# Attention in channel layout from inputs laid out by the host, one scan per tile, and a clamp moved to another engine: one core of a Trainium2 chip

## The chip, the core and the metric

The kernel runs on one core of one Trainium2 chip. TensorE (PE) does the matrix products into PSUM, VectorE (DVE), ScalarE (ACT) and GpSimd (POOL) the elementwise work, and the queue of SyncE (SP) issues most of the transfers between HBM and SBUF. The metric is the device time of the kernel in microseconds; lower is better.

## The reference

Three parts follow each other; the output of each feeds the next.

```python
# 1. attention: 4 batches, 8 heads, 768 steps, head size 48; w between 0.8 and 0.95
for t in range(768):
    cur = einsum('bhd,bhe->bhde', u * k[t], v[t])
    y[t] = einsum('bhd,bhde->bhe', r[t], state + cur)
    state = w[t][..., None] * state + einsum('bhd,bhe->bhde', k[t], v[t])
# 2. FFN on x = y as (3072 tokens, 384); w_in 384x2048 and w_out 2048x384 come as float64
h = x @ w_in
g = where(h > 0, h, exp(min(h, 0)) - 1)
x = g @ w_out
# 3. mixture of 8 experts (384 -> 1024 -> 384, ReLU), each token to its best one, times its gate weight
```

## The kernel before, in words

**Attention.** The 24 tiles are 6 chunks of 128 steps times 4 batches; tile `i` is chunk `i // 4` of batch `i % 4`. A tile runs in four steps. `A1` takes the decays with tokens on partitions, turns them with three fp32 transposes on PE (L356) into channels on partitions (128 channels, three blocks), forms running products over the later half of the chunk forwards and over the earlier half backwards in six scans of 64 columns on DVE (L359, L360), and from these the reciprocals (Ln and Exp on ACT, L367 and L368; two Newton steps, L370 and L371). It forms the product r·k·u on POOL (L382, L384), sums it by head on DVE (L385), multiplies it into v (L392) and splits v and a scaled v into fp16 high and low halves (L346 and L347). `A2` turns the decay products back with six fp32 transposes (L434, L436), multiplies them with r and k (DVE L462, in early tiles ACT L459 and POOL L460), splits these into fp16 halves (L465 and L343), makes a copy of k with the halves exchanged (L478, L479) and has three DMA transposes per tile put them with channels on partitions (RT, KT, KS). `A3` forms the scores (L507, L508), masks them (L524) and splits them (L525, L343); `A4` forms y (L551 to L553), adds what the state gives (L561, L562), hands y to the FFN as fp16 halves, and brings the state `US` up to date (L590, L597). The decay of the state over a chunk goes through `dmh` and small matmuls (L376, L377, L440, L444). The first four tiles (`EAR`) run in fp32 without DMA transposes (extra fp32 transposes, L472); tiles below `NAV` = 6 keep scores, v and the update in fp32.

**FFN.** Six groups of four tiles. `ffn_in` has 16 blocks `m` of 128 hidden channels, each of nine matmuls of 512 tokens (L608); behind each comes the ELU: `e = exp(h)` on ACT (L613), clamp and scale on DVE (L614), `max` with `h` on DVE (L615), the fp16 high half on ACT (L616), the low half on POOL (L343, `gg<-e,gg`). `ffn_out` has 192 matmuls (L628). While group g runs, the attention steps of the tiles of group g+1 are woven in; within a first group there is nothing to weave in but the start, whose four tiles follow the string `ORD`. In the first group the float64 weights are also rebuilt: three integer steps on DVE (L292 to L294), two on ACT (L306, L309), one on POOL (L310) for each of 8 + 8 pieces.

**Experts.** Blocks of 256 tokens, loaded by token number, with weights loaded per block (`SG`, `wi`) and split by ACT (L941) and DVE (L942).

A scheduler sets the order of the instructions on each engine from this program; every engine then works its list in that order and waits at semaphores. The lists of both kernels are quoted below.

Of the kernel before, what the change touches and what calls it, by code (L numbers as in the profile page):

```python
# [99 lines left out]
def _consts():  # L100
# [8 lines left out]
    d = i[None, :] - i[:, None] - 1  # L109
    put("mask", np.where(d >= 0, RHO ** np.maximum(d, 0).astype(np.float64), 0.0) * 2.0 ** (SA - 2 * SR))  # L110
    put("rt", (RHO ** (i - 128.0) * 2.0 ** (SX - SR - PG - KS_))[:, None])
    put("rv", (RHO ** (127.0 - i) * 2.0 ** SG)[:, None])
# [18 lines left out]
def body(ctx, tc, r, k, v, w, u, w_in, w_out, mod, w_gate, bias, w1, w2, cst, out, dbg=None):  # L131
# [38 lines left out]
    ubc = p1.tile([128, DM], F32, name="ubc")  # L170
    cst1 = p1.tile([128, 1], F32, name="cst1")
    cstc = cst1.to_broadcast([128, 64])
    RKs = [p1.tile([128, 2, KD, 129], F32, name=f"RK{i}") for i in range(2)]
    KXs, RXs = ([t[:, q] for t in RKs] for q in range(2))
    Rt = [p1.tile([128, H, 128], F16, name=f"Rt{i}") for i in range(2)]
    Kt = [p1.tile([128, H, 128], F16, name=f"Kt{i}") for i in range(2)]
    K2s = [p1.tile([128, H, 128], F16, name=f"K2{i}") for i in range(2)]
# [1078 lines left out]
```

## Time and profile before

| what | value |
|---|---|
| median of 3 runs | 854.38 us (853.51 to 857.72) |
| the profiled execution | 853.07 us, of which 850.8 us span from first to last instruction |
| busy in the span | PE 752.4 us (88%), DVE 607.7 (71%), ACT 488.4 (57%), POOL 394.2 (46%) |
| first `ffn_in` matmul | 65.1 us |
| first `ffn_out` | 157 us |
| later groups begin | 255.0, 343.7, 432.0, 520.9 us |
| last `ffn_in` | 545.4 to 577.6 us |
| experts | from 666 us to the end |

A busy share over the whole span mixes stages with different limits, so the rows below go by stage. Idle time of an engine matters only where another waits for what it would have done.

### The profile page before, as it was taken

How to read it: one execution, taken by the hardware profiler on the slowest of the kernel's cores; microseconds unless marked ns; L12 is line 12 of the kernel's file. 1: busy time of each engine (PE TensorE's matmuls, PEld its weight loads, DVE VectorE, ACT ScalarE, POOL GpSimd, SP SyncE). 2: the span in 40 equal slices, each digit the busy share in tenths (PEclk: the TensorE clock that was granted, in tenths of full speed). 3: DMA queues.
4: the chain of work that ended last, by engine and by line, in shares of the span. 5: the costliest groups of instructions: out<-in, count | busy, mean ns of one | idle time of the engine just before them, and what ended most of it. 6: DMA issues, size and time to landing. Idle time of an engine off the chain costs nothing.

```text
span 850.8 us, 17360 instructions
## 1 busy us (share of the span) xinstructions
PE 752.4 (88%) x6395; PEld 492.0 (58%) x6395; DVE 607.7 (71%) x1351; ACT 488.4 (57%) x1079; POOL 394.2 (46%) x397
## 2 busy tenths in 40 slices
PE   3797667899899989998999999999898799999974
PEld 2683344465456645664566455545575577777753
DVE  5659999557986699569955985297488686775751
ACT  4566667345674567455754563254474586776751
POOL 6637779635684468645763664001103622421110
PEclk9678878899999999999999899999999899999998
DMA  9937675265447453673475232115946999999920
GB/s 213 216 94 164 140 167 156 44 113 94 111 83 115 94 105 73 128 105 81 77 118 119 62 48 51 31 38 170 288 158 233 312 330 250 291 239 265 268 74 12
DMA packets 258147, 121.83 MB, mean 143 GB/s; under 512 B 221989, under 2 KB 239562, under 8 KB 258052
## 3 DMA queue, kind: packets, MB, share of 16 engines
q1 hardware_dynamic: 253728, 109.75, 55.8%
q0 software_dynamic: 3456, 10.24, 4.0%
q8 instruction: 54, 0.88, 0.4%
q10 hardware_dynamic: 868, 0.62, 0.3%
q14 instruction: 41, 0.34, 0.1%
HBM read 81.63 MB, written 9.84 MB: 108 GB/s over the span
## 4 chain that ended last, share of the span: by engine, by line
PE 33%; DVE 28%; issue 10%; DMA 10%; ACT 5%; POOL 3%; SPq 0%; POOLq 0%; DVEq 0%; ACTq 0%
PE psf L628 15%; DVE e L614 6%; PE psa L970 6%; DMA out_dram<-ob,idxb 5%; DVE e L615 4%; PE psf L950 4%; PE psf L608 3%; DMA SG<-in_moe_w_dram 3%; PE psa L950 1%; POOL gg L343 1%; DVE gb L347 1%; DVE af L524 1%; DVE W L942 1%; DVE Ab L343 1%; DVE vb L347 1%
## 5 line engine op out<-in xcount | busy, mean ns | idle before, releaser
L608 PE MATMUL psf<-xT,wi 128*128 128x512 f16 x864 | 208.6, 395 | 27.0 <-DVE sti L294 16.0
L628 PE MATMUL psf<-wo,gg 128*128 128x384 f16 x1152 | 197.2, 327 | 2.2 <-ACT gg L616 1.5
L608 PEld LDWEIGHTS <-wi 128*128 128x128 f16 x864 | 85.0, 101 | 127.2 <-issue 42.3
L628 PEld LDWEIGHTS <-gg 128*128 128x128 f16 x1152 | 110.0, 98 | 72.5 <-ACT gg L616 1.8
L343 POOL TENSOR_TENSOR gg<-e,gg 128x512 f16<-128x512 f32 x80 | 96.6, 1210 | 41.2 <-ACT gg L616 34.2
L970 PE MATMUL psa<-W,gg 128*128 128x384 f16 x624 | 106.4, 331 | 3.0 <-DVE gg L343 3.0
L950 PEld LDWEIGHTS <-W 128*128 128x128 f16 x1008 | 93.6, 99 | 19.6 <-issue 7.2
L614 DVE TENSOR_SCALAR e<-e 128x512 f32<-128x512 f32 x96 | 81.8, 852 | 17.3 <-ACT e L613 16.2
L616 ACT ACTIVATE gg<-e 128x512 f16<-128x512 f32 x96 | 60.2, 627 | 55.1 <-DVE e L615 54.8
L970 PEld LDWEIGHTS <-gg 128*128 128x128 f16 x624 | 61.5, 99 | 43.8 <-DVE gg L343 3.5
L942 DVE SCALAR_TENSOR_TENSOR W<-SG,W 128x768 f16<-128x768 f32 x56 | 52.8, 955 | 31.7 <-ACT W L941 28.0
L613 ACT ACTIVATE e<-psf 128x512 f32<-128x512 f32 x96 | 56.4, 589 | 20.6 <-POOL gg L343 12.8
L941 ACT ACTIVATE W<-SG 128x768 f16<-128x768 f32 x56 | 45.9, 836 | 37.3 <-DMA SG<-in_moe_w_dram 34.1
L615 DVE SCALAR_TENSOR_TENSOR e<-e,psf 128x512 f32<-128x512 f32 x96 | 65.0, 678 | 1.0
L942 DVE SCALAR_TENSOR_TENSOR W<-wi,W 128x768 f16<-128x768 f32 x56 | 52.3, 954 | 18.6 <-ACT W L941 14.5
L950 PE MATMUL psf<-XM,W 128*128 128x256 f16 (+1 forms) x540 | 59.5, 267 | 6.8 <-DMA XM<-G 4.9
L978 POOL DMA_INDIRECT out_dram<-ob,idxb x20 | 22.8, 1140 | 87.0 <-DVE gg L343 29.9
L941 ACT ACTIVATE W<-wi 128x768 f16<-128x768 f32 x56 | 45.4, 836 | 25.6 <-PE psa L970 15.5
L343 DVE TENSOR_TENSOR gg<-mt,gg 128x256 f16<-128x256 f32 (+1 forms) x112 | 42.1, 401 | 18.1 <-ACT gg L957 15.9
L957 ACT ACTIVATE gg<-mt 128x256 f16<-128x256 f32 (+1 forms) x112 | 40.7, 397 | 1.2
L343 POOL TENSOR_TENSOR Rt<-rkn,Rt 128x384 f16<-128x384 f32 x20 | 19.6, 980 | 42.3 <-ACT Rt L465 42.0
L956 ACT ACTIVATE mt<-psf 128x256 f32<-128x256 f32 (+1 forms) x84 | 29.2, 364 | 16.5 <-DVE gg L343 10.2
(316 smaller groups left out, 1419.2 us busy)
## 6 DMA issues: line engine op xcount, KB each, us to landing
SG<-in_moe_w_dram SPq DMA_DIRECT2D x28, 768.0 KB
wi<-in_moe_w_dram SPq DMA_DIRECT2D x28, 768.0 KB
stg<-in_moe_w_in_dram SPq DMA_DIRECT2D x8, 768.0 KB
stg<-in_moe_w_out_dram SPq DMA_DIRECT2D x8, 768.0 KB
scr<-X SPq DMA_DIRECT2D x6, 770.0 KB
lw<-in_w_dram SPq DMA_DIRECT2D x24, 192.0 KB
lr<-in_r_dram SPq DMA_DIRECT2D x24, 192.0 KB
lk<-in_k_dram SPq DMA_DIRECT2D x24, 192.0 KB
```

The costliest lines, as they stand in the source:

```text
L343: (nc.gpsimd if pool else nc.vector).tensor_tensor(lo, f, hi, op=ALU.subtract)
L608: nc.tensor.matmul(ph, lhsT=wi[:, a, kk, c0:c0 + 128], rhs=xg[:, b_ * KD + kk, :], start=(n == 0), stop=(n == 3 * KD - 1))
L613: nc.scalar.activation(e, ph, AF.Exp, scale=_pow2(-PH))
L614: nc.vector.tensor_scalar(e, e, 1.0, _pow2(PH), op0=ALU.min, op1=ALU.mult)
L615: nc.vector.scalar_tensor_tensor(e, e, -_pow2(PH), ph, op0=ALU.add, op1=ALU.max)
L616: nc.scalar.activation(gg[:, 0, m, 0:w_], e, AF.Copy)
L628: nc.tensor.matmul(po[:, 0:DM], lhsT=gg[:, a, m, 128 * i:128 * i + 128], rhs=wo[:, b_, m, :], start=(m == 0 and a + b_ == 0), stop=(m == N ...
L941: nc.scalar.activation(o_[:, 0], i_, AF.Copy, scale=_pow2(sc))
L942: nc.vector.scalar_tensor_tensor(o_[:, 1], i_, _pow2(sc), o_[:, 0], op0=ALU.mult, op1=ALU.subtract)
L950: nc.tensor.matmul(ph[:, 0:n_], lhsT=w_[:, a, kk, 128 * m:128 * m + 128], rhs=xm[:, b_ * KD + kk, 0:n_], start=(n == 0), stop=(n == 3 * KD ...
L957: nc.scalar.activation(h2[:, 0, m, 0:n_], t_, AF.Copy)
L970: nc.tensor.matmul(po[:, 0:DM], lhsT=h2[:, a, m, 128 * t:128 * t + 128], rhs=w_[:, b_, m, :], start=(m == 0 and a + b_ == 0), stop=(m == N ...
```

## The change

Attention now works with channels on partitions from the start. The host delivers r, k and w of a tile as 112 partitions (48 channels of heads 0 to 3, 16 duplicated ones, 48 channels of heads 4 to 7) by 4 head pairs by 128 steps; w has a zero column ahead of each row and its earlier half reversed. The weights of FFN and experts are laid out so that each partition reads one contiguous stretch. What the steps are now:

- `A1`: ACT doubles every fifth decay (L324); one scan of 520 columns on DVE gives all running products (L325, a vector of zeros and ones restarts it); Ln and Exp (L328, L329) and two Newton steps (L330, L331), 512 columns wide. The state's decay is one small DVE operation (L334). POOL forms r·k (L341). From tile 8 on v is split (ACT L314, DVE L315).
- `A2`: products with r and k, in two halves of 256 columns each: POOL in tiles 0 to 7 (L371), DVE afterwards (L376). PE transposes k once in fp32 (four, L381) for the update, and four small fp32 matmuls with u give the r·k·u sums (L384). From tile 8 on fp16 halves of k and r (ACT L394, POOL L311). No DMA transposes, no exchanged copy.
- `A3`, `A4`: matmuls of 48 channels that alternate between the two partition groups; three fp16 products where there were two for scores and state; y gets what the state gives in two DVE operations of 192 columns (L475); the update is 8 fp32 matmuls instead of 32 fp16 ones.
- ELU: DVE L614 goes; ACT does scale and bias instead (L514), and DVE's one operation takes `min` and `max` (L515).
- `NAV` rises from 6 to 8, and `ORD` changes.

```diff
 def A1(i):
-        for j in range(KD):
-            nc.tensor.transpose(pw[:, 128 * j:128 * j + 128], wf[:, 128 * j:128 * j + 128], cc("ident"))
-        for j in range(KD):
-            nc.vector.tensor_tensor_scan(RX[:, j, 65:129], pw[:, o + 64:o + 128], cstc, 1.0, op0=ALU.mult, op1=ALU.mult)
-            nc.vector.tensor_tensor_scan(
-                KX[:, j, 0:64][:, ::-1], pw[:, o:o + 64][:, ::-1], cstc, 1.0, op0=ALU.mult, op1=ALU.mult
+        nc.scalar.activation(lw[:, DB0::DBL], lw[:, DB0::DBL], AF.Copy, scale=2.0)
+        nc.vector.tensor_tensor_scan(flat(PR), lw, bnd, 0.0, op0=ALU.mult, op1=ALU.add)
...
-        nc.gpsimd.tensor_tensor(rk, rk, ubc, op=ALU.mult)
-        nc.vector.tensor_reduce(dg, rk.rearrange("p (h d) -> p h d", h=H), axis=AX.X, op=ALU.add)
 def A2(i):
+            if i < NAV:
...
+                for t_, xv in parts:
+                    nc.gpsimd.tensor_tensor(f[:, :, t_], xv, st[nm][:, :, t_], op=ALU.mult)
             else:
...
+                for t_, xv in parts:
+                    nc.vector.scalar_tensor_tensor(f[:, :, t_], xv, _pow2(SR), st[nm][:, :, t_], op0=ALU.mult, op1=ALU.mult)
...
+                nc.tensor.transpose(pk[:, PT * s_:PT * s_ + PT], xs[0][:, s_, :], cc("ident")[0:PT, 0:PT])
...
+            nc.tensor.matmul(pk[:, o:o + H], lhsT=st["rk"][:, s_, :], rhs=usel[:, s_, :], start=(s_ == 0), stop=(s_ == QH - 1))
...
-        transp(KT, K1.rearrange("p h x -> p (h x)"), i < NPT)
-        transp(RT, R.rearrange("p h x -> p (h x)"), i < NPT)
-        transp(KS, K2.rearrange("p h x -> p (h x)"), i < NPT)
 def ffn_in(g, m):
         nc.scalar.activation(e, ph, AF.Exp, scale=_pow2(-PH))
-        nc.vector.tensor_scalar(e, e, 1.0, _pow2(PH), op0=ALU.min, op1=ALU.mult)
-        nc.vector.scalar_tensor_tensor(e, e, -_pow2(PH), ph, op0=ALU.add, op1=ALU.max)
+        nc.scalar.activation(e, e, AF.Identity, scale=_pow2(PH), bias=nel)
+        nc.vector.scalar_tensor_tensor(e, e, 0.0, ph, op0=ALU.min, op1=ALU.max)
...
-    ORD = '00 01 10 P 02 11 P 03 12 P 20 13 30 21 31 P 22 32 P 23 33'.split()
+    ORD = '00 01 10 P 02 11 20 P 03 12 21 30 P 13 22 31 P 23 32 33'.split()
```

Three places of the engines' lists follow. The first is DVE within an `ffn_in` stretch of a middle group (`e` is the block's ELU value, `gb` the split scaled v, `RK` the decay products, `US` the state). Before:

```order
L614 TENSOR_SCALAR e<-e 128x512
L597 SCALAR_TENSOR_TENSOR US_103<-US_103,psa 112x384
L565 SCALAR_TENSOR_TENSOR y<-psa,y 128x384
L615 SCALAR_TENSOR_TENSOR e<-e,psf 128x512
L347 SCALAR_TENSOR_TENSOR gb<-lv,cs,gb 128x384
L359 SCALAR_TENSOR_TENSOR RK_92<-psa,cst_90 128x64
L360 SCALAR_TENSOR_TENSOR RK_92<-psa,cst_90 128x64
```

The same kind of place on DVE now (`rkn` is a decay product times k or r, `lw` the decays as loaded):

```order
L497 SCALAR_TENSOR_TENSOR US_98<-US_98,psa 112x192
L330 SCALAR_TENSOR_TENSOR RK_93<-RK_93,psa 112x8x64
L331 SCALAR_TENSOR_TENSOR RK_93<-RK_93,psa 112x8x64
L325 SCALAR_TENSOR_TENSOR RK_93<-lw,bnd 112x520
L376 SCALAR_TENSOR_TENSOR rkn<-RK_93,lk 112x4x64
L376 SCALAR_TENSOR_TENSOR rkn<-RK_93,lr 112x4x64
L334 SCALAR_TENSOR_TENSOR dmc<-RK_93,Z_103 112x4
L515 SCALAR_TENSOR_TENSOR e<-e,psf 128x512
```

L614 and the gb split are gone, the six short scans (two of them shown) are one long one, and the new scan and L376 read both operands from SBUF (`RK`, `lw`, `bnd`, `lk`, `lr`), where the scans read one from PSUM (`psa`).

The second place is POOL shortly ahead of the first FFN block (`wi` is a rebuilt weight piece, `x` and `ohp` the low half of y, `gg` a spare region that holds products). Before:

```order
L460 TENSOR_TENSOR gg<-gg,lr 128x8x48
L384 TENSOR_TENSOR X_99<-X_99,ubc 128x384
L460 TENSOR_TENSOR gg<-gg,lk 128x8x48
L310 TENSOR_TENSOR wi<-sti,wi 128x3x256
L392 TENSOR_TENSOR ohp<-ohp,dg 128x384
L572 TENSOR_TENSOR x<-y,x 128x384
```

POOL at the same place now (`Tk` and `Tr` belong to tiles of the next group):

```order
L371 TENSOR_TENSOR Tk<-RK_93,lk 112x4x64
L341 TENSOR_TENSOR rk<-lr,lk 112x512
L371 TENSOR_TENSOR Tr<-RK_93,lr 112x4x64
L284 TENSOR_TENSOR wi<-sti,wi 128x3x256
L398 TENSOR_TENSOR gg<-gg,dg 128x384
L371 TENSOR_TENSOR Tk<-RK_94,lk 112x4x64
L434 TENSOR_TENSOR US_98<-US_98,dmc 112x192
L479 TENSOR_TENSOR x<-y,x 128x384
```

Steps of the next group's tiles (Tk, Tr, US) now stand ahead of the first group's last x on POOL. Up to the fourth x the new list has 22 of L371 (256 columns), 5 of L341 (512), 4 of L398 and 4 of L479 (384), 3 of L434 (192) and 4 of L284 (768).

The third place is ACT within an `ffn_in` stretch. Before:

```order
L613 ACTIVATE e<-psf 128x512
L616 ACTIVATE gg<-e 128x512 x2
L613 ACTIVATE e<-psf 128x512
L444 ACTIVATE Dm_111<-psa 48x8
L346 ACTIVATE vb<-lv 128x384
L564 ACTIVATE y<-psa,cs 128x384
L613 ACTIVATE e<-psf 128x512
```

ACT now:

```order
L513 ACTIVATE e<-psf 128x512
L516 ACTIVATE gg<-e 128x512
L387 ACTIVATE kf<-psa,cs 128x448
L390 ACTIVATE dg<-psa 128x8
L514 ACTIVATE e<-e,nel 128x512
L513 ACTIVATE e<-psf 128x512
L314 ACTIVATE vb<-lv 128x384
```

ACT has three operations per block `m` instead of two, the new one (L514) with a bias from a column of SBUF, and other attention work between them.

## Rows read from the trace of the kernel before

**Rows 1.** Windows: us; busy PE, PEld, DVE, ACT, POOL; clock, DMA share, GB/s.

```profile
0.00:65.10 65.10, 43.93 (x373) 38.30 (x374) 38.69 (x115) 39.11 (x78) 38.76 (x64) 0.80 0.79 171
65.10:157.05 91.95, 62.17 (x457) 35.25 (x457) 88.51 (x160) 60.15 (x134) 72.09 (x66) 0.82 0.67 153
255.00:343.70 88.70, 83.90 (x826) 51.61 (x824) 68.30 (x151) 51.79 (x126) 53.55 (x53) 1.00 0.53 99
284.20:343.70 59.50, 54.70 (x557) 32.26 (x556) 53.01 (x121) 40.70 (x97) 42.22 (x40) 1.00 0.49 96
545.40:666.20 120.80, 108.49 (x807) 68.24 (x806) 91.54 (x287) 66.66 (x123) 17.24 (x15) 0.97 0.57 173
666.20:850.80 184.60, 168.80 (x1320) 124.28 (x1320) 116.34 (x203) 115.64 (x254) 45.59 (x39) 0.96 0.81 225
```

**Rows 2.** The chain that ended last, by line, 0 to 157 us.

```profile
by line: DVE e L614 10.8%; PE psf L608 6.6%; issue 4.0%; DVE psf L293 3.9%; DVE sti L294 3.8%; DVE psf L292 3.5%; DVE e L615 3.2%; DVE US L597 1.6%; DVE vb L347 1.5%; DVE RK L359 1.1%; DVE RK L360 1.1%; DVE gb L347 0.9%; DVE af L524 0.8%; D
```

**Rows 3.** The same chain in one ffn_in stretch.

```profile
by line: DVE e L614 11.9%; issue 10.3%; DVE e L615 9.7%; POOL gg L343 6.7%; DVE gb L347 4.5%; DVE Ab L343 4.1%; DVE af L524 4.0%; PE psf L628 3.0%; ACT gg L616 3.0%; DVE vb L347 2.9%; ACT e L613 2.7%; DVE rkn L462 2.5%; DVE RK L371 2.1%; PO
```

**Rows 4.** L614 alone in three windows: us, DVE busy.

```profile
65.10:157.05 91.95, 25.82 (x15) 0.82 0.67 153
157.05:545.40 388.35, 49.20 (x65) 0.99 0.48 88
545.40:577.60 32.20, 5.92 (x14) 1.00 0.10 32
```

**Rows 5.** L614 over the span: count, ns min/median/max.

```profile
L614 DVE TENSOR_SCALAR e<-e x96: 394/502/4485, 70.2 to 578.4; 128x512 f32<-128x512 f32 x96
```

**Rows 6.** Window of the first 42.6 us, columns as before.

```profile
0.00:42.60 42.60, 23.57 (x159) 20.10 (x161) 24.91 (x80) 23.08 (x44) 29.18 (x55) 0.84 1.03 214
```

**Rows 7.** DMA, first 42.6 us: GB/s in 40 slices; packets.

```profile
GB/s 0 47 226 305 242 209 170 196 188 186 187 188 186 215 340 341 240 160 233 394 264 195 184 166 192 173 362 288 336 379 270 154 38 146 335 335 231 60 68 129
DMA packets 26792, 9.11 MB, mean 214 GB/s; under 512 B 24588, under 2 KB 24740, under 8 KB 26788
```

**Rows 8.** Groups on POOL, 0 to 65.1 us: busy us, mean ns.

```profile
L310 POOL TENSOR_TENSOR wi<-sti,wi 128x768 f16<-128x768 f32 x5 | 8.3, 1658 | 0.8 <-ACT wi L309 0.8
...
L382 POOL TENSOR_TENSOR ohp<-lr,lk 128x384 f32<-128x384 f32 x2 | 2.0, 1006 | 4.0 <-DMA lk<-in_k_dram 4.0
```

**Rows 9.** Waits, 65.1 to 157.05 us: total, times, longest.

```profile
PE psf L608 <- DVE sti L294: 16.0, 5, 7.3
```

**Rows 10.** Groups on DVE and ACT, one period, 255 to 343.7 us.

```profile
L616 ACT ACTIVATE gg<-e 128x512 f16<-128x512 f32 x16 | 10.0, 627 | 6.2 <-DVE e L615 6.2
...
L347 DVE SCALAR_TENSOR_TENSOR gb<-lv,cs,gb 128x384 f16<-128x384 f32 x4 | 6.0, 1498 | 0.0
L343 DVE TENSOR_TENSOR Ab<-af,Ab 128x512 f16<-128x512 f32 x8 | 5.3, 680 | 0.1
...
L376 ACT ACTIVATE dmc<-RK,Z 128x1 f32<-128x1 f32 x12 | 3.4, 287 | 2.9 <-DVE RK L360 2.8
L347 DVE SCALAR_TENSOR_TENSOR vb<-lv,vb 128x384 f16<-128x384 f32 x4 | 3.3, 833 | 0.5 <-ACT vb L346 0.5
...
L359 DVE TENSOR_TENSOR_SCAN RK<-psa,cst 128x64 f32<-128x64 f32 x12 | 3.2, 266 | 1.1 <-PE psa L356 1.1
...
L346 ACT ACTIVATE gb<-lv,cs 128x384 f16<-128x384 f32 x4 | 2.4, 607 | 0.0
...
L462 DVE SCALAR_TENSOR_TENSOR rkn<-psa,lk 128x384 f32<-128x384 f32 x4 | 2.2, 553 | 8.4 <-ACT Dm L444 8.4
...
L346 ACT ACTIVATE vb<-lv 128x384 f16<-128x384 f32 x4 | 2.1, 514 | 0.0
```

**Rows 11.** Timeline of PE: start us, us, operation.

```profile
304.29 0.20 PE L551 MATMUL psa<-vb,Ab 128*128 128x48 f16 x1
304.32 0.18 PE L552 MATMUL psa<-vb,Ab 128*128 128x48 f16 x1
...
307.15 0.43 PE L440 MATMUL psa<-dmh,cs 128*48 128x8 f32 x6
```

More of the change, by code (lines that the diff above doesn't have):

```diff
@@ L57 @@
 SPC = 1.0
-NPT = 0
 NPX = 4
@@ L108, in _consts @@
     put("ident", np.eye(128))
[L109 to L112, printed above, removed]
+    before, upto = CUM[:C], CUM[1:]
+    late = i[None, :] > i[:, None]
+    put("mask", np.where(late, 2.0 ** (upto[:, None] - before[None, :]), 0.0) * 2.0 ** (SA - 2 * SR))
+    for z_ in (0, 1):
+        put(f"rt{z_}", 2.0 ** (CALL - before + SX - SR - PG - KS_ + z_ * SR)[:, None])
+        put(f"rv{z_}", 2.0 ** (upto - CALL + SG + z_ * SR)[:, None])
     put("tri", (i[:, None] < i[None, :]).astype(np.float64))
@@ L169, in body @@
     p1 = at.enter_context(tc.tile_pool(name="p1", bufs=1))
[L170 to L177, printed above, removed]
+    l3 = at.enter_context(tc.tile_pool(name="l3", bufs=3))
+    usel = p1.tile([PT, QH, H], F32, name="usel")
+    RKs = [p1.tile([PT, 2, 2, QH, HW], F32, name=f"RK{i}") for i in range(2)]
+    bnd = p1.tile([PT, 2 * QH * HW], F32, name="bnd")
+    nel = cp.tile([128, 1], F32, name="nel")
     x2a = cp.tile([128, B, XR], F32, name="X2")
@@ L312, in body @@
     z = 2 if wide else 1
[L313 to L314 removed]
+    wiv, wov = ((t.bitcast(I32) if wide else t) for t in (w_in, w_out))
     def prep_in(i):
@@ new lines, in A2 @@
+        dg = p2.tile([128, H], F32, tag="dg", name="dg")
+        nc.scalar.activation(dg, pk[:, o:o + H], AF.Copy, scale=_pow2(SX))
+        if i >= NAV:
+            for nm, f in zip("kr", xs):
+                t = p2.tile([PT, 2, QH, C], F16, tag="T" + nm, name="T" + nm)
+                nc.scalar.activation(t[:, 0], f, AF.Copy)
+                lowp(t[:, 1], f, t[:, 0], i < NLP)
+                st["t" + nm] = t
+        dv = edv[i] if i in edv else p2.tile([128, H, D], F32, tag="dv", name="dv")
@@ new lines, in A3 @@
+        pa = [psum("a") for _ in range(2)]
+        for s_ in range(QH):
+            for n in range(1 if i < NAV else 3):
+                for q in range(2):
+                    o, p_ = pa[q][:, C * s_:C * s_ + C], slice(64 * q, 64 * q + D)
+                    if i < NAV:
+                        nc.tensor.matmul(o, lhsT=KT[p_, s_, :], rhs=RT[p_, s_, :], start=True, stop=True)
+                        continue
+                    y_, z_ = LOHI[n]
+                    nc.tensor.matmul(o, lhsT=KT[p_, y_, s_, :], rhs=RT[p_, z_, s_, :], start=(n == 0), stop=(n == 2))
```

398 lines of the change are left out of this document (155 added, 243 removed).

## The prediction

> **What bounds the kernel now.** I read the stages first [rows 1]. Until 65.1 us, before the first FFN block, no engine is busy for more than 44 us of the time, but the DMA share is 0.79; in the first 42.6 us it is 1.03 [rows 6]. From 65.1 to 157.05 us, the first `ffn_in` with the rebuilding of the weights, DVE is busy 88.51 of 91.95 us: DVE is the bound. A middle group takes 88.70 us, of which PE is busy 83.90: PE is near its bound, with 4.80 us idle. The experts after 666.2 us have PE at 168.80 of 184.60 us, and little of the change reaches them.
>
> Then the chain, which says what the critical work is. Up to 157 us L614 alone, the clamp, carries 10.8% of the chain, and the three integer steps of the weights 11.2% together [rows 2]; in a later `ffn_in` stretch L614 is again first with 11.9% and L615 third with 9.7% [rows 3]. The mean hides why: L614 is 394 ns at its shortest, 502 in the median and 4485 at its longest, the same shape each time [rows 5]. In the first group it costs 25.82 us for 15, 1.72 each; behind 157 us 0.76 each; in the last group, where POOL has little to do, 0.42 each [rows 4]. So most of what it costs in the first group is waiting, not work. PE meanwhile waits 16.0 us for pieces of weights that DVE has yet to rebuild [rows 9].
>
> **The first stage, to 65.1 us.** DMA moves 9.11 MB in 42.6 us at 214 GB/s, nearly all of it in packets under 512 B, and the slices show what it can do: long stretches near 187 GB/s, others at 340 or more [rows 7]. With contiguous sources, r, k and w grow by a sixth (112 partitions of 512 instead of 128 of 384; w 520), some 10 MB in all; at 340 GB/s that is about 29 us, so the transfers cease to be the bound. Next is POOL. Its new list up to the fourth x, counted from the order above, I price by columns: 384 take 1.01 us and 768 take 1.66 [rows 8], so 256 cost about 0.78, 512 about 1.22, 192 about 0.68. 22 x 0.78 + 5 x 1.22 + 8 x 1.01 + 3 x 0.68 + 4 x 1.66 = 40 us; all of POOL's work in this stage is 38.76 us now [rows 1], so it has no less to do. POOL is busy for 29.18 of the first 42.6 us, 68% [rows 6], and for 78% of the next stage [rows 1]. At 68% its 40 us take 59, at 78% they take 51. With fewer engines in the chain of a tile (no transposes before the scan) I take 75%: 53 us, **-12**. Bounds: -6 (68%), and -23, if POOL runs at the 96% that DVE reaches in the second stage.
>
> **The second stage, to 157.05 us.** DVE loses L614: 88.51 - 25.82 = 62.7 us [rows 1, 4]. L615 stays, with the same shape. The rest of DVE's attention work changes little for these four fp32 tiles: six scans at 0.27 (1.6 us) become one, which I put at 1.1 us (at least the 0.68 us of a 512-wide operation, at most 520/64 x 0.27 = 2.2) [rows 10]; two gb splits at 1.5 go. About 60 us. POOL: per tile two r·k·u products become one (2.0 to 1.2), two products become four halves (2.0 to 3.1), four low halves of 384 (Rt, Kt, state, y sum) go (-4.0), the state's decay is half as wide (-0.3): about -4, in four tiles -16; one more weight piece falls into this stage (+1.7). 72.09 becomes about 58. ACT stays at 60: L514 replaces attention work (below). So three engines have about 60 us each, and hand to each other. At 78% (what POOL, the second engine, reaches now) the stage takes 77 us: **-15**. Bounds: -29, if the longest of them reaches 96%; -6, if only L614's undisturbed time is saved (15 x 0.394).
>
> **The middle groups, 157 to 545 us: 388.35/88.70 = 4.38 periods.** DVE per period: L614 0.76 x 16 = -12; gb -6.0; scans 24 x 0.27 = -6.4, now 4 x 1.1 = +4.4; products and sums of 384 (L462, L385) 12 x 0.55 = -6.6; 16 products of 256 with two SBUF operands at 0.45 to 0.83 (between a part of Ab's 0.68 for 512 columns, and vb's 0.83 for 384) [rows 4, 10], I take 0.62: +10. The other operations come out even. 68.30 goes to about 52, at most 60. ACT per period: 16 x L514, at L616's 0.63 plus 0.09 for an operand from a column (gb 0.607 against vb 0.514 [rows 10]), is +11.5; the doubling, kf, dg and four operations of 512 instead of 384 columns are 4 x (0.29 + 0.66 + 0.29 + 0.45) = +6.8; out go, per tile, gb, the scaled state part of y, two copies of k and eight tiny ones: 4 x (2 x 0.61 + 2 x 0.51 + 8 x 0.29) = -18.2. ACT comes out even. POOL loses some 8 of 53.55 us.
>
> PE per period: 48 records of L440 at 0.43 for six go, -3.4 us; of the other fp32 ones 36 go and some 64 come, at the same 0.07 each +2.0; of small fp16 ones 64 net go, a start every 0.03 us [rows 11], -1.9; 32 more score products of 128 columns cost about +0.8. In all -2.5. Of PE's 4.80 us idle, where it waits behind the attention's hand-overs and the ELU's buffers, I let half go with DVE's relief, since four engines are still in a block's chain (PE, ACT twice, DVE, ACT, POOL). So -5.0 per period, 4.38 x 5.0 = **-22**. Bounds: 0, and -32 (all the idle time).
>
> **Behind 545 us.** The 14 L614 that remain are 5.92 us [rows 4]; PE idles for 12 of 120.80 us in this stage [rows 1], mostly for routing and weights. I take **-2**, with -6 and +4 (L514 for 14 blocks, 10 us more on ACT, less what L614 gives up) as bounds. The experts' weights arrive in longer rows, but PE is their bound: 0.
>
> **Sum.** The profiled execution took 853.07 us, 850.8 of it span, and the median of the runs is 854.38, 0.15% above. 853.07 - 12 - 15 - 22 - 2 = **802 us**. All bounds together would be 763 and 845; the terms hardly all err to one side, so this case has 785 to 818.
>
> [...] The shortest L614 takes 0.394 us on DVE, and the same 512 columns on ACT take 0.63 or more [rows 5, 10]: undisturbed, the clamp is dearer after the move. [...]
>
> **Rivals.**
> *ACT becomes the bound (slower).* In an `ffn_in` stretch ACT is busy 40.70 of 59.50 us [rows 1]. The place is the blocks of `ffn_in`: with L514 it is up to 52 us if the attention work that ACT gives up falls outside the stretch. The gains elsewhere (12 + 15 + 2) are 29 us, so the middle groups would each have to grow by 29/4.38 = 6.6 us, the stretch to 66, ACT busy for 52/66 = 79%. Beyond that point, with waits of ACT over 14 us a stretch, the kernel is slower; at 8 us more per group, 853 - 29 + 35 = 859. Against it: ACT's sum is even, and it waits for DVE in most of its idle time (6.2 us of L616 per period [rows 10]). [...]
>
> *The waits move to the new operations of DVE.* The scan and L376 read two operands from SBUF, as gb and vb do; these take 1.498 and 0.833 us, gb's dearest by 0.67 [rows 10]. 20 such operations a period at 0.67 more are 13 us: DVE is back at 65 us, near the 68.30 of now, and PE's idle time stays, so the period gives only its 2.5 us of PE: -11. In the second stage half is lost (-7), in the first -6, behind -1: 828. [...]
>
> *Every stage reaches its floor.* The lower bounds at half to full size: 763 to 785. For it: L614 is first in both chains. Against: no stage but the second runs an engine at 96% now.
>
> **Chances.** Forecast (785 to 818) 0.54; floors 0.15; the waits on DVE (818 to 850) 0.20; within 0.5%, about what a measurement can tell from no change, 0.05 (ACT takes back about what the rest gains); ACT as the bound, slower, 0.06. So faster 0.89, same 0.05, slower 0.06. The range takes in the forecast, the floors and most of the waits on DVE: 765 to 838; the forecast's own is 785 to 818.
>
> **What would show it.** The first `ffn_in` matmul near 53 us, with DMA no longer full until 42 us, and POOL busy about 75% until then. The first `ffn_out` near 130 us, DVE no longer at 96%. Middle groups of 83 to 84 us, PE idle near 2 us, ACT busy about as before in total, and in the chain L514 with less than L614's 12%. The prediction is wrong if L325 takes over 2 us or L376 over 0.83, if ACT's L514 leads the chain, or if the first stage ends later than 59 us.

## The result, and the profile after

The changed kernel takes 841.59 us (median of 4 runs, 840.54 to 845.6), the kernel before 853.94 us in the same session: ratio 0.9861, 95% interval 0.9825 to 0.9897. Two later measurements on other chips gave 0.9869 (0.9791 to 0.9946) and 0.9862 (0.9779 to 0.9944). It is faster by some 12 us, or 1.4%; forecast were 52. The kernel before took 853 to 866 us from chip to chip, so runs below are compared within one session, or by their profiles. Medians here leave out runs more than 1.5% above the fastest of the same kernel in their session (one of e13_after, some of the kernel before).

The profiled execution took 841.33 us, 839.5 of them span. By stages, from the first matmul of each:

| stage | before | after | change | forecast |
|---|---|---|---|---|
| to the first `ffn_in` matmul | 65.1 | 80.3 | +15.2 | -12 |
| from there to the first `ffn_out` | 91.8 | 74.1 | -17.7 | -15 |
| from there to the last `ffn_out` (577.6 before, 564.1 after) | 420.7 | 409.7 | -11.0 | -22 |
| from there to the end | 273.3 | 275.4 | +2.1 | -2 |

The forecast's third term ends at 545 us, its fourth begins there; the two together were -24 and came to -8.9. Windows of the changed kernel, as in [rows 1]: us; busy PE, PEld, DVE, ACT, POOL; clock, DMA share, GB/s. Two for the first stage, the first `ffn_in`, a middle group, the rest.

```profile
0.00:40.00 40.00, 21.65 (x115) 20.11 (x116) 29.49 (x48) 15.21 (x36) 27.54 (x33) 1.00 0.81 233
40.00:80.30 40.30, 39.86 (x239) 36.71 (x238) 16.83 (x30) 15.36 (x30) 21.49 (x25) 1.00 0.25 79
80.30:154.40 74.10, 60.33 (x350) 35.31 (x350) 69.28 (x123) 51.43 (x90) 52.58 (x45) 0.91 0.45 151
239.80:328.30 88.50, 83.36 (x790) 48.91 (x789) 59.62 (x119) 53.02 (x106) 44.15 (x44) 0.96 0.29 68
564.10:839.50 275.40, 245.87 (x1932) 178.22 (x1930) 177.77 (x376) 167.83 (x351) 64.93 (x54) 0.96 0.74 221
```

The second row is the surprise: from 40 to 80.3 us PE is busy all the time, and nothing else is near it; DMA is at 0.25, as forecast, and POOL at half. The chain from 37 to 81 us, by line, and four of its pieces (start us, us, what):

```profile
by line: PE psa L449 32.0%; PE psa L416 23.8%; PE psa L489 8.1%; PE psf L355 7.4%; PE psa L384 7.0%; PE psa L381 4.3%; PE psf L384 3.5%; PE psa L464 2.3%; DVE psf L267 2.3%; DVE psf L266 2.1%; PE psf L381 1.7%; DVE RK L330 1.4%; ACT US L495
...
52.36 3.39 PE psa L449 x16
...
63.67 1.53 PE psa L384 x8
65.20 2.00 PE psa L416 x8
...
72.85 1.77 PE psa L449 x8
```

About 90% of these 44 us are PE's matmuls back to back, 83% the fp32 ones of attention: y (L449), scores (L416), update (L489), the sums with u (L384), the transposes of k (L381), what the state gives (L464). From 62.7 us on these belong to tiles of the next group, which stand ahead of the first FFN block in PE's list. The last x of the first group is turned from 69.15 to 69.65 us, and that block begins 10.7 us later; in the kernel before it began 0.9 us later (changed kernel, then the kernel before):

```profile
69.15 0.50 PE L355 MATMUL psf<-id,ohp 128*128 128x128 f16 x3
```

```profile
63.66 0.53 PE L425 MATMUL psf<-id,X 128*128 128x128 f16 x3
```

Now their price. The timeline of PE (start us, us, operation) in the first stage, and behind the first FFN blocks:

```profile
43.14 1.92 PE L449 MATMUL psa<-lv,Ab 128*128 128x48 f32 x8
44.86 0.52 PE L355 MATMUL psf<-id,x 128*128 128x128 f16 x3
...
48.52 3.09 PE L416 MATMUL psa<-gg 48*128 48x128 f32 x16 [0.44 <-ACT US L495]
...
80.33 6.27 PE L508 MATMUL psf<-xT,wi 128*128 128x512 f16 x18
...
100.86 0.77 PE L449 MATMUL psa<-lv,Ab 128*128 128x48 f32 x6
101.55 1.09 PE L464 MATMUL psa<-US,Tr 48*128 48x48 f32 x16
```

The same record (an instruction as the profile lists it) of L449 starts every 0.215 us at 43 us (1.72 us for 8) and every 0.115 us at 101 us (0.69 for 6). I call these two paces the lower and the higher level of PE's clock: in the kernel before, the records of y (L549) that start at 56 to 58 us are 0.213 us apart where the granted clock reads 0.50, and those at 44 to 45 us 0.112 us apart where it reads 1.00. The clock column of the changed kernel's windows says 1.00 for the whole first stage, at 0.215 us a record of y; the level is therefore read from the starts here. The level rose during the 18 matmuls of 512 columns that begin at 80.33 us (they start every 0.427 us until 84.57 us, every 0.216 from 84.92 us on), not during the 40 us of fp32 work ahead of them. Work in fp32 as such does not account for the lower one: in the kernel before, PE had only small matmuls in this stage too, nearly all of them fp32, and the same form of y was at the higher level at 43 us (14 records in 1.65 us, 0.118 us each):

```profile
36.23 1.97 PE L472 MATMUL psf<-cs,gg 128*128 128x128 f32 x8
37.99 2.01 PE L549 MATMUL psa<-lv,Ab 128*128 128x48 f32 x14
...
43.47 1.71 PE L549 MATMUL psa<-lv,Ab 128*128 128x48 f32 x14
```

There the level rose within the second of these lines (starts 0.213 us apart until 38.5 us and 0.112 from 38.7 us on; granted clock 0.50 from 37 to 38 us, 1.00 from 39 to 40). Which feature of the old work raised it was not tried.

In a middle group the ELU has changed as forecast, but waits have not gone. Waits of the changed kernel from 239.8 to 328.3 us (total, times, longest), and the timelines of DVE and PE around the longest of PE's:

```profile
DVE rkn L376 <- POOL Tr L311: 6.3, 3, 2.8
DVE e L515 <- ACT e L514: 5.8, 6, 2.5
PE psf L508 <- DVE e L515: 2.8, 2, 1.7
```

```profile
312.53 1.36 DVE L376 SCALAR_TENSOR_TENSOR rkn<-RK,lk 112x256 f32<-112x256 f32 x1 [2.25 <-POOL Tr L311]
313.81 1.28 DVE L428 TENSOR_TENSOR af<-psa,cs 128x512 f32<-128x512 f32 x2
...
317.35 1.30 DVE L515 SCALAR_TENSOR_TENSOR e<-e,psf 128x512 f32<-128x512 f32 x2 [0.47 <-ACT e L514]
```

```profile
309.65 4.05 PE L508 MATMUL psf<-xT,wi 128*128 128x512 f16 x18 [1.09 <-DVE e L515]
...
318.10 6.83 PE L508 MATMUL psf<-xT,wi 128*128 128x512 f16 x18 [1.69 <-DVE e L515]
```

DVE stands 2.25 us at a decay product, because both buffers of `rkn` still hold products that POOL has to read; the scores' masks, their split and L515 follow late; PE waits 1.69 us and then needs 6.83 us for 18 matmuls that took 4.05 before (granted clock 0.50 from 318.1 to 322 us; PE had been busy 1.59 of the 4 us ahead). So PE lost twice here, 1.69 us idle and 2.78 us at the lower clock behind it; the wait of 1.09 us ahead of 309.65 us was not followed by a lower clock (1.00 from 309.6 to 313.7 us).

The new operations over the whole span (count, ns min/median/max):

```profile
L325 DVE TENSOR_TENSOR_SCAN RK<-lw,bnd x24: 1233/1244/2740, 4.6 to 439.4; 112x520 f32<-112x520 f32 x24
L376 DVE SCALAR_TENSOR_TENSOR rkn<-RK,lk x32: 392/417/3593, 91.0 to 482.6; 112x256 f32<-112x256 f32 x32
L515 DVE SCALAR_TENSOR_TENSOR e<-e,psf x96: 653/686/690, 87.9 to 572.0; 128x512 f32<-128x512 f32 x96
```

L515, with one operand in PSUM, hardly varies; the two with both operands in SBUF do, by a factor of two and of nine. Of the 64 L376, the 42 with no POOL operation beside them take 0.39 to 0.43 us; all 14 that take over 0.7 us run beside POOL operations (a few others beside POOL are not slow).

### The profile page after: what moved, and what is told of

It is laid out like the page before. It is cut to its first block, busy times and chain, and to the rows that moved or that the text cites. A ratio compares the mean times of both kernels' runs of the same rounds, so it can differ in the third digit from the quotient of the medians.

```text
span 839.5 us, 16185 instructions
## 1 busy us (share of the span) xinstructions
PE 758.3 (90%) x6099; PEld 496.0 (59%) x6099; DVE 555.4 (66%) x1134; ACT 485.2 (58%) x954; POOL 341.9 (41%) x328
## 4 chain that ended last, share of the span: by engine, by line
PE 49%; DMA 16%; DVE 15%; issue 7%; ACT 6%; POOL 5%; SPq 0%; POOLq 0%; DVEq 0%; ACTq 0%
PE psf L528 19%; PE psf L508 9%; DMA out_dram<-ob,idxb 7%; PE psa L868 6%; PE psf L848 5%; DMA SG<-in_w_dram 3%; DMA stg<-in_w_out_dram 2%; DVE RK L325 2%; PE psa L449 2%; DMA lk<-in_k_dram 2%; POOL gg L311 2%; PE psa L848 2%; ACT e L514 1%; DVE W L840 1%; PE psa L416 1%
## 5 line engine op out<-in xcount | busy, mean ns | idle before, releaser
L508 PE MATMUL psf<-xT,wi 128*128 128x512 f16 x864 | 211.0, 400 | 22.0 <-DVE e L515 15.2
L528 PE MATMUL psf<-wo,gg 128*128 128x384 f16 x1152 | 193.3, 326 | 1.3 <-ACT gg L516 1.3
L311 POOL TENSOR_TENSOR gg<-e,gg 128x512 f16<-128x512 f32 x80 | 93.9, 1180 | 68.4 <-ACT gg L516 68.2
L515 DVE SCALAR_TENSOR_TENSOR e<-e,psf 128x512 f32<-128x512 f32 x96 | 65.3, 683 | 29.6 <-ACT e L514 27.4
L514 ACT ACTIVATE e<-e,nel 128x512 f32<-128x512 f32 x96 | 68.7, 719 | 1.6
L541 DVE SCALAR_TENSOR_TENSOR X<-psf,X 128x384 f16<-128x384 f32 x24 | 13.3, 556 | 71.5 <-ACT X L540 71.5
L311 DVE TENSOR_TENSOR gg<-mt,gg 128x256 f16<-128x256 f32 (+1 forms) x112 | 42.0, 402 | 18.5 <-ACT gg L855 16.4
L540 ACT ACTIVATE X<-psf 128x384 f16<-128x384 f32 x24 | 11.6, 486 | 62.8 <-PE psf L528 62.8
L341 POOL TENSOR_TENSOR rk<-lr,lk 112x512 f32<-112x512 f32 x20 | 25.7, 1286 | 42.1 <-issue 42.1
```

The lines of the kernel that those rows point to most:

```text
L311: (nc.gpsimd if pool else nc.vector).tensor_tensor(lo, f, hi, op=ALU.subtract)
L341: nc.gpsimd.tensor_tensor(rk, st["r"], st["k"], op=ALU.mult)
L508: nc.tensor.matmul(ph, lhsT=wi[:, a, kk, c0:c0 + 128], rhs=xg[:, b_ * KD + kk, :], start=(n == 0), stop=(n == 3 * KD - 1))
L514: nc.scalar.activation(e, e, AF.Identity, scale=_pow2(PH), bias=nel)
L515: nc.vector.scalar_tensor_tensor(e, e, 0.0, ph, op0=ALU.min, op1=ALU.max)
L528: nc.tensor.matmul(po[:, 0:DM], lhsT=gg[:, a, m, 128 * i:128 * i + 128], rhs=wo[:, b_, m, :], start=(m == 0 and a + b_ == 0), stop=(m == N ...
```

## Experiments

All are the changed kernel with one edit or several. The table has, from each profile, the start of the first `ffn_in` and the first `ffn_out` matmul, the three groups between the first and the fourth `ffn_out`, and the session's median and ratio to the kernel before.

| run | first ffn_in | first ffn_out | groups | median us | ratio (95%) |
|---|---|---|---|---|---|
| changed kernel | 80.3 | 154.4 | 85.4, 88.5, 88.8 | 841.6 | 0.9861 (0.9825 to 0.9897) |
| e1_warm_front | 77.7 | 159.1 | 80.1, 86.1, 88.6 | 841.9 | 0.9721 (0.9676 to 0.9767) |
| e2_warm_each | 64.9 | 154.6 | 83.8, 87.0, 87.7 | 843.1 | 0.9762 (0.9700 to 0.9824) |
| e3_clamp_dve | 80.2 | 169.1 | 81.9, 89.3, 89.0 | 856.4 | 0.9902 (0.9865 to 0.9938) |
| e4_rkn4 | 79.4 | 158.2 | 80.3, 84.7, 84.7 | 834.4 | 0.9647 (0.9601 to 0.9693) |
| e5_after | 80.6 | 158.8 | 85.6, 88.6, 88.9 | 844.4 | 0.9869 (0.9791 to 0.9946) |
| e6_p8 | 79.5 | 151.9 | 84.7, 85.7, 88.5 | 840.5 | 0.9853 (0.9804 to 0.9903) |
| e7_warm_p8 | 75.7 | 149.2 | 87.1, 87.0, 87.7 | 836.9 | 0.9788 (0.9712 to 0.9864) |
| e8_warm_p8_rkn4 | 77.0 | 151.6 | 82.5, 84.7, 84.7 | 833.0 | 0.9776 (0.9697 to 0.9855) |
| e9_nav6 | 80.0 | 164.8 | 83.0, 88.5, 86.1 | 848.9 | 0.9943 (0.9913 to 0.9973) |
| e10_two_steps | 80.7 | 151.1 | 83.9, 85.7, 88.5 | 839.3 | 0.9824 (0.9786 to 0.9862) |
| e11_warm_two_steps | 67.1 | 141.8 | 82.8, 88.2, 87.8 | 832.3 | 0.9764 (0.9720 to 0.9808) |
| e12_p8_rkn4 | 78.9 | 153.8 | 81.0, 84.7, 84.7 | 832.6 | 0.9745 (0.9696 to 0.9795) |
| e13_after | 80.0 | 154.1 | 82.8, 88.2, 86.0 | 842.5 | 0.9862 (0.9779 to 0.9944) |
| e14_rkn4 | 80.3 | 161.6 | 80.5, 84.8, 84.6 | 837.0 | 0.9734 (0.9659 to 0.9808) |
| e15_warm_rkn4 | 64.7 | 154.4 | 79.1, 84.5, 84.7 | 832.1 | 0.9678 (0.9605 to 0.9752) |
| e16_warm_p6_rkn4 | 64.7 | 144.5 | 81.3, 84.5, 84.7 | 824.2 | 0.9624 (0.9543 to 0.9706) |

Runs 1 to 4, 5 to 8, 9 to 12 and 13 to 16 each shared a chip; the kernel before took 865.6, 852.8, 854.6 and 857.1 us there. The ratios of the first four can't be set against 0.986. The changed kernel itself, profiled three times, has its first `ffn_out` at 154.1, 154.4 and 158.8 us and the next group's at 237.0, 239.8 and 244.4: differences of under 5 us at such a mark say little. A schedule also moves steps of later tiles across a mark, so a gain is worth what is left of it at a later one.

**PE's clock in the first stage.** Matmuls whose result nobody reads, on a tile of ones:

```diff
+    def warm(n):
+        pw = psum("f")
+        for _ in range(n):
+            nc.tensor.matmul(pw, lhsT=wm[:, 0:128], rhs=wm, start=True, stop=True)
 def setup():
+    nc.vector.memset(wm, 1.0)
+    warm(40)
...
     for o in ORD:
+            if o[0] in "123":
+                warm(16 if o == "12" else 6)
             at_step(int(o[0]), int(o[1:]))
```

The first run has only the 40 and the 16, the second all.

> The changed kernel with matmuls that compute nothing used: 40 fp16 matmuls of 512 columns on PE while it waits for the first data, and 16 more ahead of tile 2's second step, where it idles for 5 us. Theory A: PE ran its whole first stage at the lower clock level (fp32 records 213 ns apart, later 112), and this turned 31 us of work into 61.5. If the higher level, once reached, lasts through the fp32 work, the first ffn_in matmul moves from 80.3 to 55 to 65 us and the time from 841.6 to 817 to 828. Theory A2: fp32 work does not hold the level; records are 213 ns apart again soon after each burst, the first ffn_in matmul comes at 74 us or later, the time is 835 to 843. Theory B: the clock is not what ends the stage (POOL and DVE hand over as late); records at 112 but the first ffn_in matmul still behind 74 us.

> As the run with bursts at the front, and 6 more such matmuls ahead of every second, third and fourth step of the first four tiles (9 to 16 us of added PE work). Theory A: fp32 records 112 ns apart for nearly the whole stage, PE's first stage 31 us of its own work plus the added; first ffn_in matmul at 58 to 68 us, time 820 to 831. Theory B: records at 112, first ffn_in matmul at 74 us or later, time over 835.

With bursts at the front alone the level falls within the fp32 work: 16 records of y take 1.97 us at 30.59 us, 16 of the scores 3.06 at 34.02 and 8 of y 1.94 at 40.35, and the stage's clock column is 0.64. A2 held, first `ffn_in` at 77.7 us. With bursts before every step the clock column of the stage is 0.95, and 16 records of y take 1.88 us at 46.53 us and 1.94 at 54.37: theory A's first half held, 64.9 us; its time, 820 to 831 us, did not (843.1). The timeline of PE in e2 (its y is L458, the burst L205):

```profile
51.61 2.75 PE L205 MATMUL psf<-wm 128*128 128x512 f16 x12
54.20 0.33 PE L364 MATMUL psf<-id,ohp 128*128 128x128 f16 x3
54.37 1.94 PE L458 MATMUL psa<-gg,Ab 128*128 128x48 f32 x16
...
62.97 0.34 PE L364 MATMUL psf<-id,ohp 128*128 128x128 f16 x3 [1.37 <-POOL ohp L488]
...
64.87 2.96 PE L517 MATMUL psf<-xT,wi 128*128 128x512 f16 x13
```

16 records in the time that 8 took. The last x (62.97 to 63.31 us) comes 6.3 us earlier than in the changed kernel, with the added bursts. The other 9.1 us of the stage's gain are order: 76 matmul records of tiles 4 and 5, ahead of the first FFN block in the changed kernel, stand behind it here. And the first `ffn_out` comes no earlier, at 154.6 us. Windows of e2, first stage and first `ffn_in`:

```profile
0.00:64.90 64.90, 56.24 (x399) 36.91 (x400) 42.95 (x70) 26.45 (x56) 39.65 (x48) 0.95 0.61 176
64.90:154.60 89.70, 76.87 (x473) 47.83 (x473) 83.14 (x142) 58.64 (x108) 65.09 (x60) 0.80 0.48 149
```

All 15 us are given back in a stage that now has 473 matmul records instead of 350 (the 76 that moved, and 47 more of later tiles). DVE is busy 93% of it, as in the changed kernel, but for 83.14 instead of 69.28 us, and PE's clock column falls from 0.91 to 0.80.

**The clamp.** Back on DVE, as in the kernel before:

```diff
-        nc.scalar.activation(e, e, AF.Identity, scale=_pow2(PH), bias=nel)
-        nc.vector.scalar_tensor_tensor(e, e, 0.0, ph, op0=ALU.min, op1=ALU.max)
+        nc.vector.tensor_scalar(e, e, 1.0, _pow2(PH), op0=ALU.min, op1=ALU.mult)
+        nc.vector.scalar_tensor_tensor(e, e, -_pow2(PH), ph, op0=ALU.add, op1=ALU.max)
```

> The changed kernel with the clamp back on DVE as before (tensor_scalar, then add and max), nothing on ACT. If the move of the clamp is what shortened the stage of the first ffn_in from 91.7 to 74.1 us, the stage goes back to 84 to 92 us, DVE's tensor_scalar there is 1.2 us or more in the mean, and the time is 850 to 865. Rival: the new attention already relieves DVE, and the clamp cost only what it waited for POOL with the old work: stage within 3 us of 74, time 838 to 846.

The stage grows from 74.1 to 88.9 us, the time to 856.4. The windows of e3, the whole stage and the clamp's part of DVE alone:

```profile
80.20:169.10 88.90, 71.27 (x413) 42.89 (x413) 84.47 (x154) 48.86 (x88) 57.56 (x50) 0.79 0.46 138
```

```profile
80.20:169.10 88.90, 13.16 (x15) 0.79 0.46 138
```

The clamp takes 0.88 us in the mean, less than expected, and still decides: DVE is back at 95%. Middle groups hardly move (81.9, 89.3, 89.0). So the move of the clamp is worth 14.8 us in this stage, most of the stage's gain. Part of it is work of later tiles that e3 does within the longer stage (413 matmul records instead of 350): one group later, at 251.0 us against 239.8, 11.2 us are left (7 to 14 against the three profiles of the changed kernel).

**The buffers of the decay products.** k and r get two buffers each:

```diff
-                f = p2.tile([PT, QH, C], F32, tag="rkn", name="rkn")
+                f = p2.tile([PT, QH, C], F32, tag="rkn" + nm, name="rkn")
```

> The changed kernel with four instead of two buffers for the decay products times k and r. Theory: in the middle groups DVE stands 2.3 us at such a product until POOL has read the buffer, the ELU operation behind it comes late, PE waits 1.1 and 1.7 us and then runs some 3 us longer at the lower clock level: with more buffers these waits go, the groups of 88.5 us fall to 83 to 85, the time to 826 to 835. Rival: another hand-over takes the place of the wait, groups of 87 to 89 us, time 838 to 843.

> The changed kernel itself, as the base for the next three on one chip: 839 to 846 us, ratio 0.982 to 0.990.

> Four buffers for the decay products. If DVE's waits for these buffers cost the middle groups what their profile showed (88.5 to 84.7 us in two or three groups), 7 to 13 us less than the changed kernel beside it. If that gain came from the chip, within 3 us of it.

The wait for POOL's read is gone from the list, and the groups fall to 84.7 us with PE's clock at 1.00 and 0.98. Windows of e4, the first to be set against 239.80 to 328.30 above:

```profile
238.50:323.30 84.80, 80.06 (x790) 48.06 (x789) 59.18 (x119) 53.02 (x107) 45.80 (x44) 1.00 0.31 71
323.30:407.90 84.60, 81.56 (x788) 48.35 (x787) 58.83 (x119) 52.50 (x104) 45.76 (x44) 0.98 0.30 71
```

PE has the same matmuls in 80.06 instead of 83.36 us; its idle time falls only from 5.1 to 4.7 us in the first of these groups, and from 5.5 to 3.0 in the second (83.28 us busy of 88.80 in the changed kernel). In all six runs with four buffers these two groups take 84.5 to 84.8 us, in all eleven without 85.7 to 89.3. Side by side on one chip four buffers gave 837.0 against 842.5 us, 5.4 less, where 7 to 13 were expected. In both runs with this edit alone the first `ffn_out` came late (158.2 and 161.6 us); why was not tried.

**DVE's weight work.** In the first stage DVE is idle for 34 of 80.3 us, in the second busy for 69.28 of 74.1. More pieces of `w_in` in the first stage (the first edit for e6, e7, e8 and e12, the second for e16), or one integer step less for each:

```diff
-    ORD = '00 01 10 P 02 11 20 P 03 12 21 30 P 13 22 31 P 23 32 33'.split()
+    ORD = '00 01 10 P 02 11 20 P 03 12 21 30 P P 13 22 P 31 P 23 P 32 P 33'.split()
...
+    ORD = '00 01 10 P 02 11 20 P 03 12 21 30 P 13 22 31 P 23 P 32 33 P'.split()
...
-                nc.vector.scalar_tensor_tensor(pt, h_, -0x40000000, pt, op0=ALU.bitwise_and, op1=ALU.bitwise_or)
                 nc.vector.scalar_tensor_tensor(
-                    t[:, o:o + 384], l_, 29, pt, op0=ALU.logical_shift_right, op1=ALU.bitwise_or
+                    t[:, o:o + 384], h_, -0x40000000, pt, op0=ALU.bitwise_and, op1=ALU.bitwise_or
                 )
```

> The changed kernel itself once more, beside the next three on the same chip, since the kernel before took 854 and 866 us in different sessions. Ratio to the kernel before 0.978 to 0.992, first ffn_in matmul at 79 to 81 us, first ffn_out at 153 to 159.

> The changed kernel with all eight pieces of w_in rebuilt in the first stage instead of four (four more entries P in the order of the start). Theory: DVE, with 34 us idle in the first stage and busy 93% in the second, sets the end of the second; 13 us of DVE work move into the idle time, the first ffn_in matmul stays at 79 to 83 us, the first ffn_out comes at 140 to 147, ratio 0.968 to 0.978. Rival: PE and its hand-overs with the fp32 steps of tiles 4 to 7 set that end; first ffn_out at 151 to 158, ratio 0.980 to 0.992.

> The bursts of unused matmuls before every step together with all eight pieces of w_in in the first stage. Theory: PE's clock level set the first stage, DVE's weight work the second; with both relieved the first ffn_in matmul comes at 64 to 70 us and the first ffn_out at 126 to 136, ratio 0.950 to 0.962. If the bursts' gain is lost again whatever DVE does, first ffn_out at 145 or later, ratio over 0.970.

> The same with four buffers for the decay products. If the causes are separate, the gains add: first ffn_out at 126 to 136 us, middle groups of 84 to 85 us, ratio 0.935 to 0.950. If not, the ratio stays over 0.955.

> The changed kernel without the third integer step of the weights' rebuilding (the lowest three bits of each weight's mantissa are left out): DVE has 17.6 us less to do until the first ffn_out. If DVE sets the end of the first ffn_in, the first ffn_out comes 9 to 17 us earlier, at 138 to 147 us; if PE does, with its fp32 steps at the lower level, it stays at 150 to 158.

> The same reduction together with the bursts before every step. With bursts alone the first ffn_in matmul came at 64.9 us and the first ffn_out at 154.6, DVE busy 93% in between. If that was DVE's work, the first ffn_out now comes at 132 to 143 us. If it was PE that fell back to the lower level after 65 us, 148 or later.

> The changed kernel with four buffers for the decay products and all eight pieces of w_in in the first stage, no bursts: the two single gains (7 to 12 us and 3 to 7 us) add, first ffn_out at 149 to 155, middle groups of 84 to 85, ratio 0.960 to 0.974. If the bursts are worth something besides, it stays behind the run with all three.

Without bursts, relieving DVE gave little: 151.9 us (e6) and 151.1 (e10), the rivals' values. Their cause, PE's fp32 steps, is not shown by that. In e10 PE is busy 57.68 and DVE 59.99 of 70.4 us; PE's longest waits name DVE's last integer step of a weight piece, as in the changed kernel (e10 first, then the changed kernel from 80.3 us, with its chain by line):

```profile
80.70:151.10 70.40, 57.68 (x354) 33.37 (x354) 59.99 (x101) 51.95 (x92) 54.26 (x47) 0.85 0.53 159
```

```profile
PE psf L507 <- DVE sti L267: 11.2, 3, 5.8
```

```profile
PE psf L508 <- DVE sti L268: 6.8, 3, 3.8
```

```profile
by line: DMA stg<-in_w_out_dram 24.4%; issue 12.6%; DMA lk<-in_k_dram 7.2%; DVE psf L266 7.2%; DVE sti L268 7.1%; DVE RK L325 6.3%; DVE psf L267 6.0%; DVE e L515 4.5%; DVE Ab L425 4.4%; DVE dmc L334 3.2%; PE psf L508 2.8%; DVE RK L331 2.5%;
```

What the two engines share there is `psf`: DVE's integer steps keep their intermediate in the same four PSUM buffers that `ffn_in` fills, while the rebuilt weights (`wi`) come from ACT and POOL. And loads of the weights' float64 pieces (`stg`, two buffers) are a quarter of that chain. PSUM buffers of their own for the integer steps, or a third `stg`, are rivals that were not tried.

With bursts, one step less brought the first `ffn_out` from 154.6 to 141.8 us (e11), as expected if DVE's weight work sets that end. All eight pieces with bursts missed its expectation (e7, 149.2; e8, 0.9776): the first `ffn_in` moved back to 75.7 us, since pieces that wait for their transfer now stand ahead of the scores' masks in DVE's list (PE waits 3.0 us until 49.4 us behind such a piece, and 5.0 us for ACT's x until 37.6), and PE's clock column is 0.92 until 40 us and 0.73 from there to 80 us. Windows of e11 and of e7, first stage and first `ffn_in`:

```profile
0.00:67.10 67.10, 58.32 (x398) 37.61 (x399) 36.96 (x62) 26.78 (x56) 40.56 (x48) 0.92 0.59 170
67.10:141.80 74.70, 65.05 (x421) 39.48 (x421) 62.27 (x106) 54.33 (x100) 57.94 (x54) 0.86 0.53 165
```

```profile
0.00:75.70 75.70, 63.61 (x414) 41.43 (x414) 54.47 (x90) 32.53 (x63) 47.10 (x51) 0.84 0.66 196
75.70:149.20 73.50, 66.89 (x417) 40.33 (x415) 63.13 (x115) 52.03 (x98) 57.73 (x55) 0.85 0.40 121
```

e12 (eight pieces, four buffers, no bursts) has its first `ffn_out` at 153.8 us, as expected, and a ratio of 0.9745, just above its range and no worse than e8 (0.9776) on another chip; e6 and e7 shared a chip, 840.5 and 836.9 us. So with eight pieces the bursts add little; that they add nothing is not shown.

**Tiles 6 and 7 in fp16 halves again.** `NAV = 6`.

> The changed kernel with NAV back at 6, so tiles 6 and 7 in fp16 halves. Theory: PE's fp32 work at the lower clock level weighs in the first two stages; two tiles give back some 4 us of PE, but POOL, ACT and DVE get the splits and the products, so the first ffn_out comes at 151 to 158 us and the time stays within 4 us of the changed kernel. Rival: the fp32 steps of tiles 6 and 7 are what holds the first ffn_in; first ffn_out at 148 or earlier.

Both expectations missed: the first `ffn_out` comes at 164.8 us, 6 to 11 us later than in the changed kernel's profiles, the ratio is 0.9943. DVE is busy 83.44 of the 84.8 us of the first `ffn_in`:

```profile
80.00:164.80 84.80, 63.91 (x447) 33.56 (x447) 83.44 (x146) 61.03 (x109) 59.89 (x51) 0.81 0.46 141
```

fp32 in these two tiles is a gain here, and DVE's 83.44 against 69.28 us fits that it takes work from DVE.

**What remains open, settled side by side.** Bursts with four buffers, and the same with six pieces of `w_in` at later places:

> Four buffers and the bursts before every step. If the clock gain of the first stage is lost to DVE's weight work in the second, the first ffn_in matmul comes at 64 to 68 us, the first ffn_out at 151 to 158, and the time is within 4 us of four buffers alone. If it is kept, 10 us or more below it.

> The same with six pieces of w_in in the first stage instead of four, put at its later steps: 6.6 us of DVE work move into DVE's idle time. If DVE's weight work is what takes the gain, first ffn_in at 66 to 72 us, first ffn_out at 144 to 150, 4 to 10 us below the run with bursts and four pieces. If not, within 3 us of it.

Bursts beside four buffers gave 832.1 instead of 837.0 us, 4.9 less (within 4 were expected), with the first `ffn_out` at 154.4: the clock's gain is nearly lost. Two pieces moved into DVE's idle time brought the first `ffn_out` to 144.5 us and the time to 824.2, 8 less again, at 0.9624 of the kernel before (interval 0.9543 to 0.9706) and 18.3 us below the changed kernel beside it. Windows of the first `ffn_in` of e15, then of e16's first stage and first `ffn_in`:

```profile
64.70:154.40 89.70, 75.78 (x477) 45.79 (x477) 82.95 (x145) 59.44 (x110) 66.28 (x61) 0.81 0.48 150
```

```profile
0.00:64.70 64.70, 55.62 (x399) 36.11 (x400) 48.89 (x82) 30.33 (x61) 42.81 (x50) 0.97 0.68 201
64.70:144.50 79.80, 69.67 (x432) 43.71 (x433) 72.37 (x121) 50.85 (x93) 57.26 (x53) 0.81 0.43 134
```

DVE has 5 us more in the first stage than in e15 (43.81) and 11 less in the second; PE has 45 records fewer there too, which come later. One group later e16 is still 7.6 us ahead (225.8 against 233.4 us). e16 is the fastest version tried.

## Why the prediction was wrong

**The first stage: wrong in sign (+15.2 us instead of -12).** The step that failed is "Next is POOL". Transfers did cease to be the bound, but only behind 37 us (share 0.25 from 40 us on); ahead of that, loads of r, k and w still make up 16.7 us of the chain, the longest of them this one (start us, us):

```profile
14.49 9.47 DMA lk<-in_k_dram
```

What failed is what comes behind them: the step priced POOL's list alone and never summed PE's. PE's busy time in this stage was 43.93 us [rows 1] and is 61.51 now (21.65 + 39.86), for two reasons. The new list puts fp32 steps of the next group's tiles ahead of the first FFN block; the order quoted above shows it on POOL (Tk, Tr, US), and the prediction counted them there, not on PE. And PE stays at the lower level to the end of the stage, so each record of y costs 0.215 instead of 0.115 us; in the kernel before part of this work ran at the higher level, as its timeline of PE shows for the scores (L505), 16 records in 1.71 us where 16 of L416 take 3.09 above:

```profile
50.44 1.71 PE L505 MATMUL psa<-eRT,gg 48*128 48x128 f32 x16
```

Of the 15.2 us, about 5.5 are the later last x and the other 9.8 the steps of the next group behind it. In e2, at the higher level, the last x comes 6.3 us earlier, added bursts included; e2's other 9.1 us are the changed order. How much of the stage each reason alone would give is not shown: no run changed the order and nothing else.

**The second stage: right in the amount (-17.7 instead of -15), in part by luck.** e3 puts 14.8 us of this stage on the clamp alone, so its cause is right. The step's other part, that POOL, DVE and ACT would then be about equal, was off: DVE stays the longest with 69.28 us instead of 60, at 93% instead of the 78% that I took, two errors that nearly cancel; POOL has 52.58 instead of 58. And PE's 16.0 us [rows 9] were read as waiting for weights; the row names `psf`, and the matmul shares nothing else with that step, so it is a PSUM buffer that DVE's integer steps still use.

**The first two stages together** were forecast at -27 us and gave -2.4. A stage's end is not the sum of gains ahead of it: PE's chain holds the first stage, and DVE's weight work, with what waits for it, takes up in the second what the first gains; each engine has idle time in the other's stage. Bursts alone gave nothing at the first `ffn_out` (e2), DVE's relief alone 2.5 and 3.3 us (e6, e10), which is within the spread of the changed kernel's own profiles, both together 10 to 13 (e16, e11).

**The middle groups: right in sign, half the size (-11.0 instead of -22).** From one first `ffn_out` to the next, 87.5, 88.7, 88.7, 88.3 and 67.5 us became 85.4, 88.5, 88.8, 80.7 and 66.3: the second and third group, full ones, gained nothing, and 7.6 of the 11.0 us come from the fourth; why was not tried. The term that failed is "half" of PE's idle time. L514 costs 0.719 us in the mean, as forecast; ACT's sum is even (53.02 against 51.79 us per group); POOL fell by 9.4 us; DVE came to 59.62, at the upper bound of 60 rather than at 52: the scan takes 1.24 us undisturbed and 1.59 in the mean, L376 0.42 undisturbed and 0.74 in the mean. So DVE was relieved, and yet PE's idle time is 5.1 us a group, where it was 4.8 and 2.4 were forecast; and PE's own saving (2.5) does not show, because PE runs part of the group at the lower level: 83.36 us busy instead of 83.90. One cause is that `rkn` has two buffers that POOL reads late: the prediction counted what each operation costs, and not which buffer each waits for. e4 takes that wait away: groups of 84.7 us, where 83.7 were forecast. But most of that is busy time (80.06 and 81.56 us); idle are still 4.7 and 3.0, behind other hand-overs, of which L515 is the longest (2.1 us in the first of these groups).

**Behind them:** +2.1 instead of -2 (from a later mark than the forecast's), within the bounds given; not tried.

**The rivals.** ACT as the bound did not come: the clamp is dearer on ACT (0.719 us in the mean, against 0.394 at its shortest on DVE [rows 5]), and its move is still the largest single gain tried here. The waits on DVE's new operations with two SBUF operands are there (L325, L376, even L334, four columns, 1.03 us in the mean in the first `ffn_in`), and the time of that rival, 828, is nearer to the result than the forecast; but the larger part of the gap is PE's clock and list, which no rival named. L515 with one SBUF operand takes 653 to 690 ns throughout, while L376 with two takes 392 to 3593, and over 700 only beside POOL; what makes it long there is not shown.
